# Eight blank products in place of thirty-one, and an order worked out anew with other lengths

## The chip, the cores and the metric

The kernel runs on one core of a Trainium2 chip. A core has a matrix engine (TensorE, PE in the profile), a vector engine (VectorE, DVE), a scalar engine (ScalarE, ACT), a general engine (GpSimd, POOL) and a queue engine that issues transfers (SyncE, SP). Each works through its own list of instructions strictly in that list's order; semaphores tie the lists together. The metric is the device time of one execution, in microseconds (us).

## The reference

Two stages follow each other. The first is attention in which each query may look only at some blocks of keys: q, k and v have 4 batches, 8 heads, 768 positions and 64 numbers each, in float32. Keys are grouped in 24 chunks of 32.

```python
k_min = np.min(k_chunks, axis=3); k_max = np.max(k_chunks, axis=3)
ub = np.sum(np.maximum(q * k_min, q * k_max), axis=-1)   # one bound per query and chunk
ub = np.where(causal, ub, -1e9)
top_chunks = np.argsort(ub, axis=-1)[..., -6:]           # six chunks per query
scores = np.where(selected & causal, (q @ k.T) / 8, -1e9)
attn = softmax(scores); out = attn @ v
```

The second takes the attention's result as x, 3072 rows of 512, and computes `g = elu(x @ w_in)` with 2048 columns and `g @ w_out`, which is the output.

## The kernel before, in words

The eight heads of a batch are four pairs, so there are 16 pairs, u0 to u15; two neighbouring pairs make a quad. Positions are split in two halves of 384, called hf 0 and hf 1. Work on one batch of the attention overlaps the products of the batch before it.

The pairs of batch 0 are prepared by `first_prep` (line 619). `load` (649) brings half a pair of keys or queries, 192 KB, in one transfer; eight products with the identity matrix turn it around in PSUM (`turn`, 668, the products of line 674); ScalarE copies it out (684, 702, 707), VectorE takes minimum and maximum of each chunk (690, 697), GpSimd casts the queries (724) and the values (715). Pairs of the later batches are prepared by `pair_prep` (562): four transfers of 96 KB each for keys and for queries (572), one of 384 KB for values (613), a transpose on VectorE (585, 603), minimum and maximum on VectorE (589), casts on GpSimd (724).

`quad_sel` (727) computes the bounds on TensorE (`ub`, 756), and VectorE finds each query's sixth largest bound and marks the chunks below it (773 to 796). GpSimd puts the marks below the queries (807), as further rows, so that the product of queries and keys (`sc`, 848) comes out already masked; each tile of keys carries 24 rows made from the constant `econ` for that (512). `pair_attend` (828) takes exponentials on ScalarE (875), masks the diagonal on GpSimd (894) or, early on, by a further product (854), multiplies by v (907), divides on VectorE (920, 923), transposes on TensorE (932) and copies the result to `xT` on ScalarE (935). `mlp` (939) multiplies by w_in, 16 blocks of 128 columns (`up`, 957), computes elu on ScalarE and VectorE (967 to 1001), and multiplies by w_out (`down`, 1020); ScalarE copies the result out and SP stores it (1028, 1032). The weights are brought by transfers that GpSimd issues (`weights`, 537, lines 541 and 545), each tied by `gates` to a step of the attention.

The order of all this isn't written by hand. Each step is handed to a `Plan` (128) with an engine, an assumed length, a priority, and what it reads and writes. `Plan.order` (191) first shifts the priorities by the list `RANKS` (first step, count, shift in fiftieths), and then lets a model of the engines and of the transfers take steps one by one: on each engine the step that can start first, and among those that can start at once the one of the lowest priority number. Buffers and PSUM banks are given out in the same pass. In the model, transfers stop in the stretches named in `STALLS` (140). The steps are then emitted in the order found, and that is the order of every engine's list. Where the assumed lengths differ from the chip's, the lists remain as they are, and an engine waits for whatever its next step lacks.

Ahead of all steps stand the blank products (lines 1081 to 1087): VectorE clears a tile, and TensorE multiplies it by itself into a PSUM bank that nobody reads.

The lines that the profile names are printed here.

Of the kernel before, what the change touches and what calls it, by code (L numbers as in the profile page):

```python
# [12 lines left out]
F32 = mybir.dt.float32  # L13
# [4 lines left out]
S = 768  # L18
# [23 lines left out]
def WHEN(q_in, left, out):  # L42
# [7 lines left out]
WARM = 31  # L50
# [5 lines left out]
RANKS = ((2, 1, 127), (6, 1, -127), (13, 1, -97), (17, 1, -112), (31, 1, -89), (35, 1, -71), (48, 1, -89),  # L56
# [62 lines left out]

DUMP = None  # L120


class Op:
    __slots__ = ("eng", "dur", "lat", "emit", "deps", "prio", "alloc", "free", "n", "users",
                 "left", "ready", "start", "end", "tag", "after", "followers", "port", "dma", "issues", "lane")


class Plan:
# [8 lines left out]
    COLD = 7.0  # L137
    RING = 2560
    LANES = 8
    STALLS = ((9.6, 11.7),)  # L140
    WAKE = 1.8

    def __init__(self, caps):
# [228 lines left out]
def kernel(  # L372
# [707 lines left out]
    with tc.manual_schedule():  # L1080
        if WARM:
# [4 lines left out]
            for _ in range(WARM):  # L1086
                nc.tensor.matmul(nothing, lhsT=blank, rhs=blank, start=True, stop=True)
# [34 lines left out]
```

## Time and profile before

| What | Value |
|---|---|
| Median of three runs | 276.94 us (276.51 to 277.29) |
| The profiled execution's own time | 276.84 us |
| Its span, first to last instruction | 275.1 us |
| TensorE busy | 264.6 us |
| VectorE busy | 202.0 us |
| ScalarE busy | 203.1 us |
| GpSimd busy | 127.4 us |
| Bytes moved by transfers | 29.82 MB |

1.7 us of the profiled execution lie outside the span. A row of the profile names a line of the kernel, an engine, an operation and its tiles; "idle before" is the time that the engine stood still just ahead of it, and the arrow names what ended that. Waits matter only on an engine that is the bound of its stretch. TensorE's records of neighbouring products overlap, because a product's end lies after the start of the next one.

### The profile page before, as it was taken

What the parts mean: (1) busy time and instruction counts of PE and PEld (TensorE: products, weight loads), DVE (VectorE), ACT (ScalarE), POOL (GpSimd) and SP (SyncE); (2) the same over time, 40 slices, a digit from 0 to 9 for tenths busy, and PEclk for the clock granted to TensorE, in tenths of its full rate; (3) what the DMA queues carried; (4) which work ended last, traced back from release to release, by engine and by line L of the source; (5) the groups of instructions that cost most, each with busy time, mean ns of one, the idle gap of its engine ahead of it and who ended that gap; (6) DMA issues with size and microseconds to landing.
All of it is one profiled execution on the core that took longest, in us unless ns stands there. A gap on an engine that the chain in (4) does not pass through costs nothing.

```text
span 275.1 us, 7274 instructions
## 1 busy us (share of the span) xinstructions
PE 264.6 (96%) x2751; PEld 164.7 (60%) x2751; DVE 202.0 (73%) x546; ACT 203.1 (74%) x382; POOL 127.4 (46%) x235
## 2 busy tenths in 40 slices
PE   8889899999999998999999999999999999999995
PEld 8778566565666564655566556665566755554544
DVE  5874979969999969999994775677965379374420
ACT  3879899948996898878999979964589844433311
POOL 5768565756997795968676164100162100000000
PEclk9999999999999999999999999999999999999999
DMA  7999999999999999999691010101020000210222
GB/s 184 240 222 230 174 165 179 158 160 156 191 156 151 173 149 179 196 158 174 94 212 42 2 38 2 38 0 41 1 80 0 28 13 2 77 38 2 76 76 76
DMA packets 111474, 29.82 MB, mean 108 GB/s; under 512 B 101072, under 2 KB 108496, under 8 KB 111440
## 3 DMA queue, kind: packets, MB, share of 16 engines
q1 hardware_dynamic: 106800, 24.78, 47.8%
q0 software_dynamic: 4224, 4.19, 9.6%
q8 instruction: 21, 0.34, 0.6%
q10 hardware_dynamic: 416, 0.39, 0.5%
q14 instruction: 13, 0.11, 0.1%
HBM read 27.26 MB, written 6.29 MB: 122 GB/s over the span
## 4 chain that ended last, share of the span: by engine, by line
PE 59%; DVE 21%; DMA 8%; ACT 5%; issue 3%; SPq 2%; POOL 1%; DVEq 0%; POOLq 0%
PE psM L1020 14%; PE psH L957 13%; PE psS L848 8%; PE psS L957 8%; PE psMT L1020 8%; DMA stage<-in_q_dram 5%; PE psO L907 4%; DVE thr L785 3%; DVE gT L975 2%; DVE qt L603 2%; SPq L572 2%; DVE selv L790 1%; ACT pt L875 1%; DVE gT L1001 1%; DVE ubt L773 1%
## 5 line engine op out<-in xcount | busy, mean ns | idle before, releaser
L875 ACT ACTIVATE pt<-psS 128x768 bf16<-128x768 f32 (+1 forms) x120 | 90.8, 789 | 5.8 <-PE psS L848 3.8
L957 PE MATMUL psH<-xT,w_in_sb 128*128 128x384 bf16 x384 | 74.0, 326 | 2.7 <-DVE gT L975 1.0
L1020 PE MATMUL psM<-w_out_sb,gT 128*128 128x512 bf16 x288 | 71.3, 379 | 0.0
L957 PEld LDWEIGHTS <-w_in_sb 128*128 128x128 bf16 x512 | 48.1, 97 | 38.1 <-issue 5.0
L967 ACT ACTIVATE e<-psH 128x384 f32<-128x384 f32 x96 | 48.1, 508 | 14.7 <-PE psH L957 14.1
L1020 PEld LDWEIGHTS <-gT 128*128 128x128 bf16 x400 | 37.4, 97 | 33.5
L894 POOL TENSOR_SCALAR_AFFINE_SELECT pt<-pt 128x256 bf16<-128x256 bf16 (+1 forms) x56 | 29.0, 522 | 57.3 <-ACT pt L875 56.2
L848 PE MATMUL psS<-rhs,lhs 88*128 88x384 bf16 (+4 forms) x304 | 52.5, 284 | 1.6 <-DVE ubt L773 0.6
L848 PEld LDWEIGHTS <-lhs 88*128 88x128 bf16 x304 | 27.4, 97 | 16.0 <-issue 2.1
L996 DVE SCALAR_TENSOR_TENSOR t<-e,psH 128x384 bf16<-128x384 f32 x48 | 25.7, 543 | 13.3 <-ACT e L967 13.2
L907 PEld LDWEIGHTS <-pt 128*128 128x128 bf16 x672 | 28.2, 98 | 6.7 <-issue 0.3
L724 POOL CAST rhs<-qt 64x768 bf16<-64x768 f32 (+1 forms) x40 | 27.7, 696 | 9.1 <-ACT qt L702 4.1
L807 POOL COPY rhs<-selt 24x192 bf16<-24x192 bf16 (+2 forms) x56 | 25.4, 455 | 13.6 <-DVE selt L796 9.5
L975 DVE SCALAR_TENSOR_TENSOR gT<-e,psH 128x384 bf16<-128x384 f32 x48 | 25.4, 535 | 8.0 <-ACT psH L972 7.3
L907 PE MATMUL psO<-vext,pt 128*128 128x65 bf16 x672 | 31.2, 194 | 0.0
L1001 DVE SCALAR_TENSOR_TENSOR gT<-psH,t 128x384 bf16<-128x384 f32 x48 | 25.9, 547 | 0.8
L967 ACT ACTIVATE e<-psS 128x768 f32<-128x768 f32 x16 | 13.0, 810 | 17.4 <-PE psS L957 17.4
L972 ACT ACTIVATE psH<-psH 128x384 f32<-128x384 f32 x48 | 24.7, 524 | 0.0
L957 PE MATMUL psS<-xT,w_in_sb 128*128 128x384 bf16 x128 | 23.1, 326 | 0.0
L1020 PE MATMUL psMT<-w_out_sb,gT 128*128 128x512 bf16 (+1 forms) x112 | 22.4, 349 | 0.0
L985 DVE TENSOR_SCALAR t<-e 128x768 bf16<-128x768 f32 x16 | 8.9, 559 | 16.8 <-ACT e L967 16.6
L724 POOL CAST lhs<-kt 64x768 bf16<-64x768 f32 x24 | 19.6, 818 | 2.0 <-PE psS L848 1.1
(66 smaller groups left out, 297.5 us busy)
## 6 DMA issues: line engine op xcount, KB each, us to landing
out_dram<-osb SPq DMA_DIRECT2D x23, 256.0 KB, 2.0
stage<-in_q_dram SPq DMA_DIRECT2D x48, 96.0 KB, 4.5
stage<-in_k_dram SPq DMA_DIRECT2D x48, 96.0 KB, 3.5
vd<-in_v_dram SPq DMA_DIRECT2D x12, 384.0 KB, 5.4
w_in_sb<-in_moe_w_in_dram POOLq DMA_DIRECT2D x4, 512.0 KB, 9.5
w_out_sb<-in_moe_w_out_dram POOLq DMA_DIRECT2D x4, 512.0 KB, 8.3
gT<-in_v_dram SPq DMA_DIRECT2D x16, 96.0 KB, 5.9
gT<-in_k_dram SPq DMA_DIRECT2D x6, 192.0 KB, 4.9
```

The source lines that it names most:

```text
L724: nc.gpsimd.tensor_copy(out=o, in_=i)
L807: eng.tensor_copy(out=dst.rearrange("c h (i two x) -> c h i two x", two=2, x=32)[:, :, :, odd, :], in_=tiles[st][r0:r0 + NCH, c0:c0 + n].r ...
L848: nc.tensor.matmul(p_s[:, hd, pc:pc + w], lhsT=tiles[pt_["kb"]][0:64 + NCH, hd, 128 * kb:128 * kb + 128], rhs=tiles[pt_["qb"]][0:64 + NCH, ...
L875: lambda bs=bs, pt=pt, wtot=wtot, lo=lo, at=at: nc.scalar.activation(out=tiles[pt][:, :, lo:lo + wtot], in_=tiles[bs[0]][:, :, at:at + wto ...
L894: nc.gpsimd.affine_select(out=a, in_=a, compare_op=AOT.is_ge, fill=0.0, base=0, pattern=pat, channel_multiplier=-1)
L907: nc.tensor.matmul(po[:, hd, qi, :], lhsT=tiles[pt][:, hd, off:off + 128], rhs=tiles[pt_["vx"]][:, 6 * hd + kb, :], start=(kb == 0), stop= ...
L957: nc.tensor.matmul(ph, lhsT=w_in_sb[:, kk, f0:f0 + 128], rhs=tiles[XT[4 * b + kk]][:, c0:c0 + HALF], start=(kk == 0), stop=(kk == NKK - 1))
L967: lambda e=e, view=view: nc.scalar.activation(out=tiles[e][:, 0:step], in_=view(), func=AF.Exp),
L975: lambda e=e, view=view, fc=fc, gt=gt: nc.vector.scalar_tensor_tensor(out=tiles[gt][:, fc:fc + step, :], in0=tiles[e][:, 0:step], scalar=1 ...
L996: lambda e=e, t=t, view=view: nc.vector.scalar_tensor_tensor(out=tiles[t][:, 0:step], in0=tiles[e][:, 0:step], scalar=1.0, in1=view(), op0 ...
L1001: lambda t=t, view=view, fc=fc, gt=gt: nc.vector.scalar_tensor_tensor(out=tiles[gt][:, fc:fc + step, :], in0=view(), scalar=0.0, in1=tiles ...
L1020: nc.tensor.matmul(pm, lhsT=tiles[gt][:, fc, 128 * tt:128 * tt + 128], rhs=w_out_sb[:, fc, cs], start=(fc == 0), stop=(fc == NFC - 1))
```

## The change

`WARM` is 8 in place of 31, and the blank products take 512 columns in place of 128, so the cleared tile grows from 128 to 512 columns and the bank's tile with it. The lengths that the plan assumes are altered for the early loads (issue 0.43 in place of 0.5, a half of keys or queries 0.069 in place of 0.062), for the values' casts, the bounds, and the products with w_in and w_out. The transfers' stops are put at five other times. `RANKS` is another list of shifts (386 entries before, 294 after, nearly all different). No step's own work is altered, and none is added or taken away beside the blank products.

```diff
-WARM = 31
+WARM = 8
-RANKS = ((2, 1, 127), (6, 1, -127), (13, 1, -97), (17, 1, -112), (31, 1, -89), (35, 1, -71), (48, 1, -89),
...
+RANKS = ((2, 1, -127), (4, 1, -23), (13, 1, -62), (15, 1, -90), (17, 1, -117), (19, 1, -127), (29, 1, -53),
...
-    STALLS = ((9.6, 11.7),)
+    STALLS = ((11.3, 13.0), (66.0, 67.0), (74.0, 75.0), (82.0, 82.6), (91.0, 91.6))
...
-        fetch(0.5, pl + 1.2, vload, [vd], (0.022, 1536, 1), alloc=[vd], reads=late)
-        add("POOL", 0.13 + 0.00084 * S, pr + 1.0,
+        fetch(0.43, pl + 1.2, vload, [vd], (0.022, 1536, 1), alloc=[vd], reads=late)
+        add("POOL", 0.14 + 0.00086 * S, pr + 1.0,
...
-        fetch(0.5, pl, load(at_k, kw, nc.sync), [(hk, i0)], (0.062, 192, 1), alloc=ak)
-        fetch(0.5, pl + 0.1, load(at_q, qw, nc.scalar if early else nc.sync), [(hq, i0 + 1)], (0.062, 192, 1),
+        fetch(0.43, pl, load(at_k, kw, nc.sync), [(hk, i0)], (0.069, 192, 1), alloc=ak)
+        fetch(0.43, pl + 0.1, load(at_q, qw, nc.scalar if early else nc.sync), [(hq, i0 + 1)], (0.069, 192, 1),
...
-        add("POOL", 0.13 + 0.00084 * HALF, pr + 1.0,
+        add("POOL", 0.14 + 0.00086 * HALF, pr + 1.0,
...
-        add("POOL", 0.13 + 0.00084 * w, pr, f, **kw)
+        add("POOL", 0.14 + 0.00086 * w, pr, f, **kw)
...
-            add("PE", 0.22 + 0.002 * n, pr, ub, reads=rd, writes=[bu[0]], alloc=bu, free=fr)
+            add("PE", 0.27 + 0.00166 * n, pr, ub, reads=rd, writes=[bu[0]], alloc=bu, free=fr)
...
-                add("PE", step * 4 * 0.1625, pr, up,
+                add("PE", step * 4 * 0.1618, pr, up,
...
-                        add("PE", 4 * (0.0033 + wide / 2400), pr, down,
+                        add("PE", 4 * (0.0024 + wide / 2400), pr, down,
...
-            blank = const.tile([P, P], BF16, name="blank")
-            nothing = psum.tile([P, P], F32, name="nothing", tag="bank3")
+            blank = const.tile([P, 512], BF16, name="blank")
+            nothing = psum.tile([P, 512], F32, name="nothing", tag="bank3")
             nc.vector.memset(blank, 0.0)
             for _ in range(WARM):
-                nc.tensor.matmul(nothing, lhsT=blank, rhs=blank, start=True, stop=True)
+                nc.tensor.matmul(nothing, lhsT=blank[:, 0:P], rhs=blank, start=True, stop=True)
```

What this does to each engine's list, as it comes out when both kernels are built:

- POOL, start: before, the identity (483) stands ahead of the two selections that make `econ` (500, 502); after, behind both of them. On VectorE the clearing of the query tiles (507) moves behind the three constants (474 to 476).
- SP, start: the third keys' load moves ahead of the first values and of the third queries. In the second half of batch 0 all keys and queries are loaded ahead of the last eight values' loads.
- POOL, batch 0: the cast of the third pair's values goes between the two casts of the fourth pair's queries.
- TensorE, batch 0: the turn of the queries of pair u2, second half, moves from the middle of the attention to just ahead of the first product with w_in.
- SP, batch 1: the four loads of u5's queries go ahead of the first 384 KB of values (613), not behind them.
- Batches 1 to 3: the order of keys' and queries' loads, of transposes and of products is different almost throughout. The bounds of u10 and u11 come 17.7 us of TensorE work later, those of u14 and u15 25.8 us of work earlier.

108 rows, old and new, of the table RANKS are left out of this document.

## The prediction

> **What bounds the kernel now.** I read the page first, then the busy time by stretches of 12 us, then the chain of waits, and last the order in time at the front and at three waits.
>
> ```profile
> span 275.1 us, 7274 instructions
> PE 264.6 (96%) x2751; PEld 164.7 (60%) x2751; DVE 202.0 (73%) x546; ACT 203.1 (74%) x382; POOL 127.4 (46%) x235
> DMA  7999999999999999999691010101020000210222
> PE 59%; DVE 21%; DMA 8%; ACT 5%; issue 3%; SPq 2%; POOL 1%; DVEq 0%; POOLq 0%
> ```
>
> TensorE is busy for 264.6 of 275.1 us, so 10.5 us of idle time is all that any order can win, and not all of that: the first product starts at 1.06 us and the last output's store follows the last product. The change leaves the work as it is. What it can do is move, shrink or enlarge these 10.5 us. The busy time by stretches (columns: stretch, length, busy and instructions of PE, its weight loads, DVE, ACT, POOL, clock, DMA share, GB/s) shows where they lie.
>
> ```profile
> 0.00:12.00 12.00, 10.10 (x155) 9.39 (x157) 8.80 (x27) 6.58 (x14) 7.62 (x26) 1.00 0.98 206
> 12.00:24.00 12.00, 10.88 (x247) 9.34 (x245) 7.96 (x37) 10.14 (x26) 9.06 (x19) 1.00 1.18 234
> 24.00:36.00 12.00, 11.07 (x155) 7.56 (x154) 8.91 (x34) 10.98 (x24) 8.14 (x17) 1.00 1.14 181
> 36.00:48.00 12.00, 11.13 (x145) 7.52 (x145) 11.17 (x35) 11.97 (x25) 6.95 (x14) 1.00 1.17 176
> 60.00:72.00 12.00, 11.68 (x126) 6.56 (x114) 11.26 (x42) 9.83 (x20) 9.05 (x17) 1.00 1.05 167
> 96.00:108.00 12.00, 11.12 (x166) 6.73 (x163) 8.92 (x38) 10.66 (x22) 8.78 (x13) 1.00 0.96 156
> 108.00:120.00 12.00, 11.65 (x163) 7.25 (x162) 11.88 (x32) 9.79 (x20) 10.09 (x17) 1.00 1.09 185
> 120.00:132.00 12.00, 11.35 (x77) 6.33 (x75) 11.94 (x33) 10.72 (x20) 8.96 (x19) 1.00 0.98 171
> ```
>
> ```profile
> 30.00:125.00 95.00, 91.32 (x1050) 55.69 (x1050) 86.03 (x256) 81.75 (x156) 70.19 (x121) 1.00 1.04 167
> ```
>
> TensorE stands still for 1.90, 1.12, 0.93 and 0.87 us in the first four stretches, 0.32 in 60 to 72, and 0.88, 0.35 and 0.65 in 96 to 132. From 132 us on there is no wait worth a line: TensorE then has more work waiting than it can do, and a better order wins nothing. Up to there the transfers are always busy, and VectorE nearly so; its one large gap (8.92 of 12) goes with the chain's wait for a load:
>
> ```profile
> 48.67 9.92 DMA stage<-in_q_dram
> ...
> 97.60 3.56 DMA stage<-in_k_dram
> ```
>
> **The change part by part.** The order is told by the two lists; "work ahead" is a count over a list, each instruction at its mean length in this profile.
>
> (1) The front: blanks, identity.
>
> ```profile
> 0.90 0.11 DVE L1085 MEMSET blank<- 128x64 uint32 x1 [0.90 <-PEq L1106]
> 1.06 3.49 PE L1087 MATMUL nothing<-blank 128*128 128x128 bf16 x31 [1.06 <-DVE blank L1085]
> 1.10 1.05 DVE L507 MEMSET rhs<- 32x192 uint32 x5
> ...
> 2.17 0.36 POOL L497 MEMSET vext<- 128x12 bf16 x5
> 2.46 0.29 POOL L483 TENSOR_SCALAR_AFFINE_SELECT ident_f<-ident_f 128x128 f32<-128x128 f32 x1
> 3.39 0.29 POOL L479 TENSOR_SCALAR_AFFINE_SELECT trineg<-trineg 128x128 bf16<-128x128 bf16 x1 [0.64 <-DVE trineg L476]
> 3.63 0.81 POOL L500 TENSOR_SCALAR_AFFINE_SELECT econ<-econ 32x768 bf16<-32x768 bf16 x1
> ...
> 4.48 1.55 PE L674 MATMUL psH<-ident_f,gT 96*64 96x96 f32 x16
> 4.52 0.81 POOL L502 TENSOR_SCALAR_AFFINE_SELECT econ<-econ 32x768 bf16<-32x768 bf16 x1
> 5.82 0.98 PE L674 MATMUL psMT<-ident_f,gT 96*64 96x96 f32 x16
> ```
>
> A memset of 64 elements takes 0.11 us, of 192 (1.05 by 5) 0.21; 256 make 0.26 by that line, so the blanks begin 0.15 later. 31 blanks of 128 columns fill 1.06 to 4.48, at most 0.11 each; eight of 512 at four times that make 3.5, which is as much. They end near 4.7. The identity now comes after two selections: the memsets ahead end at 2.5, the selections stand 0.89 apart, so 2.5 + 2 x 0.89 + 0.29 = 4.6. Both end near 4.7, and the first turn starts 0.3 later: **+0.3**. Ends: 0 (the first turn was held by its load) and +0.9 (the selections only start at 3.4, where the trineg selection of before still waited for VectorE).
>
> (2) The third keys' load comes three issues earlier on SP.
>
> ```profile
> 6.63 0.83 PE L674 MATMUL psH<-ident_f,gT 96*64 96x96 f32 x16
> ...
> 8.75 0.88 PE L674 MATMUL psH<-ident_f,gT 96*64 96x96 f32 x16 [0.63 <-ACT qt L702]
> 9.83 0.88 PE L674 MATMUL psMT<-ident_f,gT 96*64 96x96 f32 x16 [0.20 <-DVE kx L690]
> ```
>
> The named releaser of the 0.63 had long ended, so it was the load. This wait goes; behind it ScalarE, which copies each turn out, is the next to be late: its list has the same steps up to the first exponentials and starts later by (1). I take **-0.2**; ends 0 and -0.83 (both waits).
>
> One hole in the loads moves too. Of the early loads of 96 KB those issued at 6.9 to 8.5 land after 4.3 us, the one of 8.6 to 9.05 after 5.8 (transfers on those tiles by the stretch of their issue), and 8 to 14 us has one fetch of instructions in this queue (packets, MB, share):
>
> ```profile
> DMA to landing us min/median/max: 4.3/4.3/4.4
> ```
>
> ```profile
> DMA to landing us min/median/max: 5.7/5.8/5.9
> ```
>
> ```profile
> q8 instruction: 1, 0.02, 1.3%
> ```
>
> [...] Going by the row, 46 instructions fewer on TensorE (23 blanks with their weight loads), where a turn's 32 take 0.88 us, put the hole some 1.3 us later, behind the first keys of the second half instead of on values. Those are turned only after two scores: **0**; ends 0 and +0.8.
>
> (3) On POOL a cast of values (L715, 0.5 us) now stands between the two casts that the fourth pair's first scores need, and the bounds of that quad stand behind these scores on TensorE. In return the marks of the first pair are no longer split by such a cast. **0**; ends -0.5 and +0.5.
>
> (4) One turn (0.88) moves to just ahead of the first product with w_in.
>
> ```profile
> 28.65 0.88 PE L674 MATMUL psMT<-ident_f,kt 96*64 96x96 f32 x16 [0.31 <-ACT xT L935]
> 29.62 0.34 PE L932 MATMUL psT<-ident_b,on 128*128 128x128 bf16 x3
> 30.45 0.81 PE L957 MATMUL psH<-xT,w_in_sb 128*128 128x384 bf16 x4 [0.49 <-DVE kx L690]
> ```
>
> Between the transpose and the product, which wait on ScalarE's copy to xT, TensorE stands for 0.49; a turn of 0.88 fills that. **-0.5**; ends 0 and -0.8 (both waits).
>
> (5) u5's queries are issued ahead of 384 KB of values.
>
> ```profile
> 44.81 0.53 SPq L613 DMA_DIRECT2D vd<-in_v_dram  x1
> 45.44 12.82 SPq L572 DMA_DIRECT2D stage<-in_q_dram  x8
> ```
>
> ```profile
> 58.66 0.98 DVE L603 STREAM_TRANSPOSE qt<-stage 128x768 f32<-128x768 f32 x1 [1.53 <-DMA stage<-in_q_dram]
> ```
>
> This is the 9.92 of the chain. At 167 GB/s, 384 KB are 2.4 us. The transpose comes that much earlier, but TensorE is full in 48 to 60 and idle for only 0.32 in the next stretch. **-0.3**; ends 0 and -0.32. The values, behind the queries, are late next; nothing multiplies by them until that quad's scores.
>
> (6) Batches 1 and 2. The load waited for at 97.60 belongs to u10's keys. In the new lists it has 1.15 MB (7.1 us at 167 GB/s) more loads ahead, but 10.1 us more VectorE work ahead of its transpose: 3.0 us more cover, about what VectorE stood there (12 - 8.92 = 3.08). The bounds of u8 and u9's second half come 7.8 us, and u10 and u11's 17.7 us of TensorE work later. Against it: u8's keys lose 3.4 us of cover, u13's queries 7.1. The idle of 96 to 132 is 0.88 + 0.35 + 0.65 = 1.88. Most of these waits are products with w_in whose bank VectorE hasn't freed, and VectorE's total stays; so I take about half, **-1.0**; ends 0 and -1.88.
>
> (7) The rest. VectorE's preparation of u14 and u15 must be ready 25.8 us of TensorE work earlier; the count leaves 24 us of TensorE work over VectorE's there, where the tightest places have 10. In the end phase the products with w_in of the last half follow the last transpose after 0.86 us of other products, where (4) showed 30.45 - 29.62 = 0.83 needed. **+0.1**; ends 0 and +0.5. Shorter assumed lengths have no cost of their own.
>
> Sum: 0.3 - 0.2 + 0 + 0 - 0.5 - 0.3 - 1.0 + 0.1 = -1.6. On the profiled execution's own time, 276.84: **275.2 us**. That execution is 0.1 below the median of 276.94, so nothing is to be corrected. All low ends make -4.3, all high ends +3.0; both at once are unlikely.
>
> **The rivals.** *Nothing nets out, 276.8.* Up to 132 us VectorE is busy for 11.2 to 11.9 of 12 in most stretches; if it holds TensorE there by its sum of work, a wait that goes at one place comes back at the next one, and (4) to (6) are paid back. For it speaks that 86.03 of 95 are busy; against it, that TensorE's idle time is largest where VectorE too stands (96 to 108), so both wait for loads.
>
> *Slower, by the front, 277.8.* The identity comes after both selections; if they start at 3.4, the first turn starts at 5.4, +0.9. ScalarE is busy for 10.14 and 10.98 of 12 in the stretches after and passes the delay on up to the first product with w_in. With (4) and (2) used up by that, 276.84 + 0.9 = 277.8. It decides as soon as the identity comes after 5. Against it: VectorE's constants now come first, so the selections needn't wait for it.
>
> *Slower, by a load, 278.3.* Transposes of u8's keys or u13's queries reach the head of VectorE's list before their loads; behind them stand the steps that free the banks of the products with w_in. The like of it at 58.66 held VectorE for 1.53. In a stretch where TensorE has no other work that is 276.84 + 1.5. It decides where the 3.4 or 7.1 us of lost cover exceed what was there; by the count some 9 us remain.
>
> *The best case, 273.4:* (2), (4) and (6) at their low ends, 275.2 - 0.6 - 0.3 - 0.9 = 273.4.
>
> [...] The first turns of 16 products start at 4.48, 5.82 and 6.63, so 1.34 and 0.81 apart: the second ran faster. [...]
>
> **How the numbers follow.** Forecast, 274.4 to 276.0: 0.48. Best case: 0.08. Nothing nets out, 276.1 to 277.7: 0.20. The front: 0.14. A load: 0.10. A measurement of this kernel tells 0.3%, 0.83 us, from no change: faster means below 276.1. So faster 0.56, within 0.20, slower 0.24. The range takes in the best case and the load: 273.4 to 278.3.
>
> **What would show it.** (1) First turn near 4.8, identity at 4.6. (2) No wait of 0.6 at the fifth turn. (4) No wait of 0.49 ahead of the first product with w_in. (5) The last of u5's queries transposed by 56. (6) TensorE idle in 96 to 132 below 1.2, VectorE's gap in 96 to 108 smaller. The forecast is wrong if TensorE's idle time up to 132 us isn't below the 8 us or so of before, wherever it then lies.

## The result, and the profile after

The changed kernel takes 275.82 us (median of 22 runs, 274.56 to 280.48), the kernel before, run beside it, 277.79 (22 runs). The ratio is 0.9927, with a 95% interval of 0.9905 to 0.995: faster by 0.73%, some 2.0 us, where 1.6 were forecast. The profiled execution has 275.80 us with a span of 274.1, against 276.84 and 275.1, so the two traces compared here differ by 1.0 us only. Some executions of each kernel show a lower mean granted clock and last longer (the changed kernel's two longest, 280.48 and 280.46 us, have 0.988, where those under 276 have 0.998 to 1.000; one of the kernel before, beside a later run, 282.95 us at 0.962); the ratios leave most of them out.

First the page of the changed kernel: span, TensorE's busy time (matmuls and weight loads), and the summary of its chain of waits.

```profile
span 274.1 us, 7208 instructions
PE 263.4 (96%) x2705; PEld 163.0 (59%) x2728; DVE 200.4 (73%) x546; ACT 200.7 (73%) x382; POOL 127.7 (47%) x235
PE 80%; DMA 6%; ACT 3%; POOL 3%; DVE 3%; issue 2%; SPq 1%; ACTq 0%; POOLq 0%; DVEq 0%
```

VectorE's share of the chain fell from 21% to 3%. TensorE's busy time can't be compared directly: 2705 matmuls are on record beside 2728 weight loads, so the records of 23 matmuls are missing, and each may show as a small hole. The same stretches of 12 us as in the prediction:

```profile
24.00:36.00 12.00, 10.50 (x171) 7.14 (x175) 8.24 (x33) 10.48 (x23) 6.10 (x12) 1.00 1.09 180
48.00:60.00 12.00, 10.86 (x111) 6.83 (x110) 9.68 (x17) 10.29 (x20) 6.02 (x10) 1.00 1.11 175
96.00:108.00 12.00, 11.89 (x128) 7.14 (x127) 10.09 (x26) 11.17 (x22) 9.74 (x16) 1.00 1.04 177
108.00:120.00 12.00, 11.95 (x141) 7.76 (x140) 11.93 (x37) 10.18 (x22) 7.80 (x15) 1.00 1.19 170
120.00:132.00 12.00, 11.94 (x105) 7.24 (x104) 11.04 (x21) 12.00 (x24) 11.31 (x19) 1.00 1.14 163
```

In 96 to 132, where 1.88 us stood idle, 0.22 do. VectorE's gap in 96 to 108 is 1.91 where it was 3.08, and most of it, 1.79 at 103.01, is now a wait for TensorE and not for a load. But 48 to 60, which had none, has lost 1.14. The order in time shows where (TensorE, POOL, VectorE and a piece of the chain, sorted by start):

```profile
1.26 3.60 PE L1071 MATMUL nothing<-blank 128*128 128x512 bf16 x8 [1.26 <-DVE blank L1069]
4.17 0.28 POOL L467 TENSOR_SCALAR_AFFINE_SELECT ident_f<-ident_f 128x128 f32<-128x128 f32 x1
4.79 1.55 PE L658 MATMUL psH<-ident_f,gT 96*64 96x96 f32 x16
29.59 0.34 PE L916 MATMUL psT<-ident_b,on 128*128 128x128 bf16 x3 [0.83 <-DVE selv L774]
44.69 8.08 DMA stage<-in_k_dram
45.33 1.51 POOL L529 DMA_DIRECT2D w_out_sb<-in_moe_w_out_dram  x2
52.89 0.98 DVE L569 STREAM_TRANSPOSE kt<-stage 128x768 f32<-128x768 f32 x1 [1.24 <-DMA stage<-in_k_dram]
54.37 1.02 PE L1004 MATMUL psM<-w_out_sb,gT 128*128 128x512 bf16 x3 [0.96 <-DVE gT L985]
58.48 0.98 DVE L587 STREAM_TRANSPOSE qt<-stage 128x768 f32<-128x768 f32 x1 [0.40 <-DMA stage<-in_q_dram]
```

POOL issues the second pair of loads of w_out at 45.33, where the kernel before did so at 47.99. The last quarter of u5's keys, issued 0.64 us ahead of it at 44.69, lands only after 8.08 us. VectorE comes to the transpose of these keys, waits 1.24, and the step that makes gT stands behind it; TensorE waits 0.96 for that step.

To follow such losses through different orders I use one more number, the **shortfall**: the start of a weight load, less the length of all TensorE work that stands before it in the program. Lengths are those of packed runs in the traces: columns at 2.4 per ns and 2.5 ns more for each product, which gives the 0.65 of four with 384 columns (179.13 to 179.78 in the changed kernel) and the 0.86 of four with 512 (164.26 to 165.12), 0.032 us for a product with values, 0.83 for a turn (9.00 to 9.81), 0.39, 0.70 or 1.13 for a set of bounds. Where TensorE is full the shortfall stays level; what it grows is time lost. In us, by the time in the trace:

```
at (us)          25     50     60     92    124    132    268
before         4.57   8.15   8.31  10.85  14.40  14.55  15.37
changed        4.62   8.64  10.38  12.16  12.57  12.62  14.17
```

The change loses 2.07 by 60 us, wins 0.76 up to 92 and 3.24 from there to 132, and loses 0.73 after: 1.20 won in all. One trace stands for each kernel here, and two traces of one list can differ by microseconds, as k10_early below shows; so a shortfall is read for where it grows, and the ratios for what an edit is worth in all.

### The profile page after: what moved, and what is told of

Read it like the earlier page. It is cut to its first block, busy times and chain, and to the rows that moved or that the text cites. A ratio compares the mean times of both kernels' runs of the same rounds, so it can differ in the third digit from the quotient of the medians.

```text
span 274.1 us, 7208 instructions
## 1 busy us (share of the span) xinstructions
PE 263.4 (96%) x2705; PEld 163.0 (59%) x2728; DVE 200.4 (73%) x546; ACT 200.7 (73%) x382; POOL 127.7 (47%) x235
## 3 DMA queue, kind: packets, MB, share of 16 engines
q0 software_dynamic: 4224, 4.19, 9.5%
## 4 chain that ended last, share of the span: by engine, by line
PE 80%; DMA 6%; ACT 3%; POOL 3%; DVE 3%; issue 2%; SPq 1%; ACTq 0%; POOLq 0%; DVEq 0%
PE psM L1004 21%; PE psH L941 18%; PE psS L832 10%; PE psS L941 8%; PE psMT L1004 8%; PE psO L891 7%; PE psS L740 4%; DMA stage<-in_k_dram 3%; ACT pt L859 2%; DMA gT<-in_q_dram 2%; PE psT L916 2%; DMA gT<-in_k_dram 2%; PE psMT L658 1%; POOL lhs L708 1%; PE psH L658 1%
## 5 line engine op out<-in xcount | busy, mean ns | idle before, releaser
L1004 PE MATMUL psM<-w_out_sb,gT 128*128 128x512 bf16 x269 | 68.3, 379 | 2.0 <-DVE gT L985 1.0
L951 ACT ACTIVATE e<-psH 128x384 f32<-128x384 f32 x96 | 48.4, 524 | 10.6 <-PE psH L941 10.2
L791 POOL COPY rhs<-selt 24x192 bf16<-24x192 bf16 (+2 forms) x56 | 25.5, 456 | 16.4 <-DVE selt L780 13.8
L980 DVE SCALAR_TENSOR_TENSOR t<-e,psH 128x384 bf16<-128x384 f32 x48 | 25.8, 544 | 8.5 <-ACT e L951 8.5
L919 ACT ACTIVATE xT<-psT 128x384 bf16<-128x384 bf16 x32 | 16.4, 511 | 7.3 <-PE psT L916 7.3
```

The source lines that it names most:

```text
L791: eng.tensor_copy(out=dst.rearrange("c h (i two x) -> c h i two x", two=2, x=32)[:, :, :, odd, :], in_=tiles[st][r0:r0 + NCH, c0:c0 + n].r ...
L951: lambda e=e, view=view: nc.scalar.activation(out=tiles[e][:, 0:step], in_=view(), func=AF.Exp),
L980: lambda e=e, t=t, view=view: nc.vector.scalar_tensor_tensor(out=tiles[t][:, 0:step], in0=tiles[e][:, 0:step], scalar=1.0, in1=view(), op0 ...
L1004: nc.tensor.matmul(pm, lhsT=tiles[gt][:, fc, 128 * tt:128 * tt + 128], rhs=w_out_sb[:, fc, cs], start=(fc == 0), stop=(fc == NFC - 1))
```

## The experiments

Ratios are against the kernel before, run on the same chip, with 95% intervals. Where an order is rewritten, a list of operation numbers takes the place of the planner's walk; the rest of the kernel stays as it is. The new shifts and the new lengths can't be had apart: with old shifts and new lengths, or new shifts and old lengths, the planner comes to a point where no operation can start. So how much of the result belongs to either stays open.

**The two halves of the order exchanged at 58 us.**

```
- steps = plan.order()
+ steps = walk(plan, ORDER)   # front_before: before's list where start < 58, then the changed list
+                             # front_after: the changed list where start < 58, then before's
```

> The order of before up to 58 us of its plan, and what is left in the order of the changed kernel. Theory (the change wins some 3.3 us between 60 and 135 us and loses 2.2 between 40 and 58): ratio to before 0.985, about 273.6 us where the changed kernel has 275.8; TensorE waits in 48 to 60 as before, in 96 to 132 as the changed kernel. Rival (the gain comes from the front, the blanks aside): ratio 1.000, as before. Rival (only the whole order hangs together, loads out of step at the seam): slower than the changed kernel, ratio over 0.993.

> The reverse: the order of the changed kernel up to 58 us, and what is left in the order of before. Theory: the 2.2 us lost by 58 us stay lost and nothing is won later, ratio to before 1.008, and the waits of 96 to 132 are back (1.9 us). Rival (the gain comes from the front): ratio 0.993, as the changed kernel.

Measured: front_before 0.996 (0.9935 to 0.9985), front_after 1.0068 (1.0033 to 1.0102). The later part of the new order, seam included, is worth 0.4% behind the old front and 1.41% (1.0068 - 0.9927) behind its own; the new front by itself costs 0.68%. The 0.985 expected of front_before was a miss:

```
at (us)          25     50     60     92    124    132    268
front_before   4.58   8.26   9.50  12.47  13.06  13.11  14.72
front_after    4.62   8.47  11.55  13.94  15.59  16.00  16.77
```

From 92 to 132 us it loses 0.64, nearly as little as the changed kernel's 0.46, and front_after 2.06. That is less than the 3.70 of before, though each engine has the very list of before there. What differs is that the loads are in time: VectorE's waits of before for them (1.34 and 1.87; the first two lines) are gone, TensorE's of 0.29, 0.59 and 0.19 with them, and only the later ones are left (the third line is of front_after; before has the same 0.42 at 122.53).

```profile
97.02 0.98 DVE L603 STREAM_TRANSPOSE qt<-stage 128x768 f32<-128x768 f32 x1 [1.34 <-DMA stage<-in_q_dram]
101.24 0.98 DVE L585 STREAM_TRANSPOSE kt<-stage 128x768 f32<-128x768 f32 x1 [1.87 <-DMA stage<-in_k_dram]
124.04 1.46 PE L941 MATMUL psH<-xT,w_in_sb 128*128 128x384 bf16 x8 [0.42 <-DVE gT L985]
```

So 1.64 of the 3.24 won in this stretch can be had without the new list, from loads in time alone (here they are in time because all runs some 3 us later); the other 1.60 comes with the new list. But front_before was to keep the 8.31 of before at 60, and by 92 it is at 12.47. Its waits, on VectorE and TensorE:

```profile
58.63 0.98 DVE L587 STREAM_TRANSPOSE qt<-stage 128x768 f32<-128x768 f32 x1 [1.37 <-DMA stage<-in_q_dram]
60.35 0.34 PE L916 MATMUL psT<-ident_b,on 128*128 128x128 bf16 x3 [1.34 <-DVE on L907]
61.84 0.37 PE L740 MATMUL psS<-qa,km 64*32 64x96 f32 x8 [0.69 <-ACT qa L590]
```

The load of u5's queries is as late as in the kernel before (58.66, a wait of 1.53), where it cost TensorE nothing. At the seam a division that TensorE needs next stands behind it on VectorE, and TensorE waits 1.34: a front and a rest fit together only through their loads.

**The same exchange at 90 us.**

```
+ # changed_to_90: the changed list where start < 90, then before's; before_to_90 the reverse
```

> The order of the changed kernel up to 90 us of its plan, and what is left in the order of before. Theory (the win sits behind 90 us): TensorE stands 12.2 behind its work at 92 as in the changed kernel, and loses 4.5 more up to the end, as before did, where the changed kernel loses 2.0: ratio to before 1.001. Rival (the win sits between 58 and 90, or comes from the whole order): 0.993 to 0.996.

> The reverse: the order of before up to 90 us, what is left in the order of the changed kernel. Theory (the win sits behind 90 us and can be had without the loss at 55): TensorE 10.9 behind at 92 as before, and 2.0 more up to the end: ratio to before 0.988, 274.6. Rival (the later order needs the loads that its own first part has issued by then; the seam costs what is won): 0.994 or more, with new waits for loads between 90 and 110.

Measured: 1.0257 (1.0192 to 1.0321) and 1.0296 (1.0262 to 1.033). Both are far slower than either kernel, and the rival of before_to_90 stands. In changed_to_90 and then before_to_90 TensorE shows

```profile
104.85 1.44 PE L832 MATMUL psS<-rhs,lhs 88*128 88x384 bf16 x4 [5.42 <-POOL rhs L791]
```

```profile
100.27 0.34 PE L891 MATMUL psO<-vext,pt 128*128 128x65 bf16 x3 [4.34 <-POOL pt L878]
96.00:108.00 12.00, 7.27 (x49) 4.14 (x51) 7.12 (x13) 5.80 (x9) 6.36 (x12) 0.72 0.77 137
```

so nothing on the place of the win can be read from them; they show only what a seam costs where two lists differ in which pair comes next. Behind both long waits stand loads, as that rival has it: the chain of changed_to_90 goes back from POOL to a load of values, 5.66 us from 95.37, and in before_to_90 POOL waits 2.8 us for VectorE's transpose of queries, and that one 1.9 for its load.

**One transpose put back.** The place of the win needed a smaller cut. The changed kernel transposes u10's keys at 111.46 without a wait, 4 us after they land.

```
  VectorE's list: ..., ubt, gT,
+   kt of u10 (keys transposed),
    max, gT, selv, kt of u12, selt, gT, t, gT, gT, km of u12, t,
-   kt of u10,
    reciprocal, ...
```

> The changed kernel with one thing undone: VectorE's transpose of u10's keys moved ahead in its list past ten steps, to the place at 105.9, where their load (landing at 107.46) is not there yet, as in the kernel before; all loads as they are. Theory (the win between 92 and 132 us is VectorE no longer standing for loads ahead of steps that free the banks of products with w_in): VectorE waits 1.5 to 2 there, TensorE stands for gT about as long, is 1 to 2 us more behind at 124 us than 12.57, ratio to before 0.997 to 1.000. Rival (such a wait costs nothing by itself, VectorE's total or the order of its steps does): 0.993, TensorE at 124 us as the changed kernel.

Measured: 1.0089 (1.0052 to 1.0126). From 100 to 124 us its shortfall grows from 15.80 to 19.02, by 3.22, where the changed kernel's grows from 12.17 to 12.57. VectorE's wait and the one that follows on TensorE:

```profile
111.75 0.98 DVE L569 STREAM_TRANSPOSE kt<-stage 128x768 f32<-128x768 f32 x1 [1.93 <-DMA stage<-in_k_dram]
113.63 0.81 PE L941 MATMUL psH<-xT,w_in_sb 128*128 128x384 bf16 x4 [2.30 <-DVE gT L959]
```

One step of VectorE too early for its load, by 1.93, costs TensorE 2.30 at once, and 2.8 by 124 us (3.22 less the 0.40 of the changed kernel): the theory holds for the place, and the price is above the 1 to 2 expected. The ratio says more than the edit costs: this profile had lost 3.45 more than the changed kernel before 60 us, where the lists are the same (see the last section), so the ratio of 0.997 to 1.000 that was expected is missed, by a loss that this trace has ahead of the edit; why k10_early has it stays open. The reverse was tried on the kernel before:

```
  VectorE's list of before: ...,
-   kt of u10,
    ubt of u8 and u9,
-   km of u10,
    max of u8 and u9,
-   kx of u10,
    reciprocal, gT, on,
+   kt, km, kx of u10,
    gT, ...
```

On POOL the cast of these keys goes behind a cast of values with them, since it needs what VectorE makes.

> The kernel before with one move: VectorE's transpose of u10's keys and its two reductions behind seven other steps (bounds of u8 and u9, a division, products' steps) of its list, as the changed kernel has them later. Theory (the win of 92 to 132 us is VectorE no longer standing for loads): VectorE's wait of 1.87 at 101.2 shrinks below 0.5, TensorE's wait of 0.59 at 105.3 goes, ratio to before 0.995 to 0.997. Rival (VectorE's total, not the wait, holds TensorE there): ratio 1.000, the time comes back in waits for gT by 132.

Measured: 1.0102 (1.0045 to 1.0159), a miss. But most of what the trace lost was lost ahead of the move: at 50 us its shortfall is some 5.4 above that of before, in steps where the lists are the same, and TensorE's granted clock is down there (the figure ahead of the last two):

```profile
16.00:20.00 4.00, 4.00 (x76) 3.29 (x74) 2.26 (x13) 2.11 (x5) 2.18 (x6) 0.61 1.20 222
20.00:24.00 4.00, 4.00 (x42) 3.45 (x42) 1.64 (x6) 2.70 (x6) 1.44 (x4) 0.50 1.21 221
```

What the move itself does is read from 92 to 132 us, where the shortfall grows by 4.7 and that of before by 3.7: 1.0 lost, where a gain was expected.

```profile
109.60 0.97 DVE L585 STREAM_TRANSPOSE kt<-stage 128x768 f32<-128x768 f32 x1
112.93 0.81 PE L957 MATMUL psH<-xT,w_in_sb 128*128 128x384 bf16 x4 [1.99 <-DVE gT L975]
```

VectorE's wait of 1.87 for the load is gone, as expected. But the three steps (0.97, 0.95 and 0.94) now stand, by the place I chose, directly ahead of a step that makes gT, and TensorE waits 1.99 for that, where it waited 0.59. So it isn't enough that VectorE never waits for a load: at this place other work ahead of the step that frees the bank costs TensorE more than the wait did.

**The loss at 55: the loads of w_out.**

```
  POOL's list: ...,
-   second w_out pair,
    km of u4, mask, cast of u4's keys,
+   second w_out pair,
    casts of u4's queries, ...
```

> The changed kernel with the second pair of loads of w_out issued three of POOL's instructions later, at about 48.4 us where it is 45.3 (before: 48.0). Theory (this stream holds up the loads of u5's keys): the keys land 1 to 2 us earlier than 52.8, TensorE's wait of 0.96 at 54.4 goes, ratio to before 0.988. Rival (the keys' load is late by its own issue, or the products with the second half of w_out now wait): ratio 0.993 or more, and a wait of products with w_out for their load near 58.

Measured: 0.9908 (0.9876 to 0.994), and a span of 272.5. The pair is issued at 46.30, not at 48.4, but that is 2.2 us behind the last quarter of the keys (issued at 44.10) and is enough:

```profile
46.30 1.53 POOL L529 DMA_DIRECT2D w_out_sb<-in_moe_w_out_dram  x2
51.09 0.97 DVE L569 STREAM_TRANSPOSE kt<-stage 128x768 f32<-128x768 f32 x1
48.00:60.00 12.00, 11.87 (x152) 7.43 (x149) 9.86 (x19) 9.88 (x19) 6.67 (x10) 1.00 1.21 172
```

From issue to landing the last two quarters of u5's keys took, in the changed kernel (the first line) and here (the second),

```profile
DMA to landing us min/median/max: 3.7/5.9/8.1
```

```profile
DMA to landing us min/median/max: 4.0/4.0/4.1
```

and the shortfall at 60 us is 8.92 where the changed kernel has 10.38. No product with w_out waits for its load. In the profile it stays 1.5 ahead to the end (12.64 against 14.17); the timed runs don't tell 0.9908 from 0.9927. In w_out_turn below, with the same move, the last two quarters take 4.0 and 3.8 us.

**The step behind the late load.**

```
  VectorE's list: ..., t,
-   kt of u5, gT,
+   gT, kt of u5,
    reciprocal, ...
```

> The changed kernel with VectorE's transpose of u5's keys moved behind one step, the gT step that stood behind it in the list (loads as they are). Theory (the late load costs TensorE time only through this place in VectorE's list): the wait of 0.96 at 54.4 goes; TensorE at 60 us 0.5 to 1 us ahead of the changed kernel; ratio to before 0.990. Rival (up to 60 us the loads set the time, and the wait comes back at the next place): ratio 0.993, and the same 10.4 us behind its work at 60.

Measured: 0.9928 (0.9898 to 0.9958). The wait at 54.4 goes and comes back at the next place:

```profile
54.63 0.98 DVE L569 STREAM_TRANSPOSE kt<-stage 128x768 f32<-128x768 f32 x1 [1.83 <-DMA stage<-in_k_dram]
57.12 0.34 PE L916 MATMUL psT<-ident_b,on 128*128 128x128 bf16 x3 [1.10 <-DVE on L907]
```

The shortfall at 60 is 11.34, no better. The rival holds: the load is what has to be moved.

**The blanks alone.**

```
-WARM = 8
+WARM = 31
-                nc.tensor.matmul(nothing, lhsT=blank[:, 0:P], rhs=blank, ...)
+                nc.tensor.matmul(nothing[:, 0:P], lhsT=blank[:, 0:P], rhs=blank[:, 0:P], ...)
```

> The changed kernel with 31 blank products of 128 columns in place of eight of 512; everything else as it is. Theory (the same total of blanks, nothing else): ratio to before 0.993 and the first turn within 0.2 of 4.79. [...]

> The kernel with the later w_out loads, and 31 blank products of 128 in place of eight of 512. With 31 blanks the changed kernel stood 0.91 at 22.45, waiting for nothing the profile shows, and was 1.2 us later at 25 us, but lost that lead at 55 anyway. Theory (46 instructions more put an instruction fetch on TensorE's path there, and the load of u5's keys had hidden it): the same wait near 22, and now it reaches the end: ratio 0.995 where the eight blanks have 0.991. Rival (the blanks are worth nothing): 0.991.

Measured: 0.9937 (0.991 to 0.9964), and with the later w_out loads 0.9939 (0.9911 to 0.9967), where the eight blanks gave 0.9927 and 0.9908. The first turn is at 4.68. The end hardly moves, but the middle does: the shortfall of blanks_31 is 5.83 at 25 us, 9.78 at 50, and 10.46 at 60 beside the changed kernel's 4.62, 8.64 and 10.38. In blanks_31 TensorE has

```profile
22.45 0.32 PE L891 MATMUL psO<-vext,pt 128*128 128x65 bf16 x5 [0.91 <-issue]
```

a wait for nothing that the profile shows; w_out_blanks31 has it too (1.21 at 22.39), and the changed kernel has no such wait there. The traces don't tell what it is: from 18 to 23 us blanks_31 and the changed kernel have the same fetches of instructions, one packet on q8 and one on q14. The expectation that it would reach the end at 0.995 once the later w_out loads took its cover away is neither borne out nor excluded: the intervals overlap.

**The moved turn.**

```
  TensorE's list: turn of u3's queries,
+   turn of u2's queries,
    transpose (psT),
-   turn of u2's queries,
    first product with w_in, ...
```

> The changed kernel with the moved turn of u2's queries one place further ahead on TensorE, before the transpose that waits 0.83 at 29.6 for VectorE's division. Theory for the place: that wait is filled, the first product with w_in comes 0.7 earlier, at 30.0. Theory for the end (the loads of u5 hold the kernel at 55 us): ratio to before 0.993 all the same. Rival (gains before 55 us last): ratio 0.990.

> Two single moves on the changed kernel together: the second pair of w_out's loads three of POOL's instructions later, and the turn of u2's queries one place further ahead on TensorE. Theory: the late w_out keeps the keys' load ahead of the stream, so the 0.4 to 0.8 won at 30 us by the turn now last: ratio to before 0.989. Rival (what is won before 55 us is lost by 60 to the loads): 0.991, as with the later w_out alone.

Measured: 0.9941 (0.991 to 0.9972), and with the later w_out loads 0.9924 (0.9894 to 0.9954): no gain from either, and both theories for the place fell. In turn_ahead:

```profile
29.21 0.88 PE L658 MATMUL psMT<-ident_f,stage 96*64 96x96 f32 x16 [0.68 <-DVE selv L774]
30.95 2.11 PE L941 MATMUL psH<-xT,w_in_sb 128*128 128x384 bf16 x12 [0.58 <-ACT xT L919]
```

The turn waits for VectorE as well (until the step of line 774 ends at 29.03; its queries had landed by 20.8), so it is not work that was ready. And the product that it had covered now waits for ScalarE's copy again.

## Why the prediction was right, and where its terms were not

The total was right, -2.0 by the runs where -1.6 was forecast, but as a sum of terms that went wrong in both directions: a loss of 2.07 where -0.3 stood, and a gain of 3.24 where -1.0 stood. That they cancel so well is luck. Two of its sums don't come out of its own figures: the high ends add up to +2.7, not +3.0, and the idle time of before up to 132 us is 7.1, not "8 us or so". It set as its test that this idle time falls; it is 6.3 in the changed kernel.

(1) The front: right. Blanks to 4.86, the identity at 4.45 (4.17 + 0.28), the first turn at 4.79, 0.31 later. The rival of a slow front, which needed the identity behind 5, falls with that. (2) The wait ahead of the fifth turn is gone, though the seventh now waits 0.41 for its keys, at 10.81, and the shortfall at 20 us is 3.83 where before had 4.23: terms (1) and (2) together gave -0.4, not +0.1. The hole in the loads, costed at 0, cost nothing that the changed kernel's trace shows; no run shows that a fetch of instructions makes it, or that fewer instructions move it. The traces show q8's packet at 11.0 us before and at 13.8 in the changed kernel, 2.8 later where 1.3 was estimated, and the step up in the time to landing at the load of 96 KB issued at 8.63 before (from 4.3 to 5.7) and at one of 192 KB issued at 10.69 in the changed kernel (from 5.1 to 6.3). Part (2) put the hole into the loads alone, and blanks_31 has a wait of 0.91 on TensorE itself without a releaser. That this wait is a fetch of instructions is argued, from its coming with 46 more instructions; no row names it. (3) No wait that belongs to it was found.

(4) Failed. "A turn of 0.88 fills that": the wait of 0.49 ahead of the first product went, but 0.83 stands ahead of the transpose at 29.59, and that product starts at 30.68, not before the old 30.45. turn_ahead shows why: the turn isn't ready work, it waits for VectorE too.

(5) Failed, with the wrong sign. The last of u5's queries are transposed at 58.48, not by 56. The step counted what stands ahead on SP's queue only. The same new order issues the second w_out pair 2.7 us earlier, on POOL's queue, and beside that stream the keys' last quarter lands only after 8.1 us (4.0 to 4.1 in w_out_later), the queries after 7.1 to 8.2. POOL's queue was left out of that step. Instead of -0.3 the stretch to 60 us gave +2.07 by the shortfall. w_out_later, one trace, takes 1.46 of it back.

(6) Right in its mechanism, and far too small: -1.0 was taken, -3.24 came between 92 and 132 us. k10_early shows the mechanism by putting the wait back: VectorE's wait for a load becomes TensorE's wait for a bank, 1.93 to 2.30. front_after shows how much of the win it can be: without VectorE's waits for loads the list of before wins 1.64. The other 1.60 comes with the order of the new list, and which of its steps bring it wasn't followed. The cover came out at 4 us against a wait of 1.87 before, a gain of 5.9 where 3.0 was counted. The size failed for one more reason, in the measure: the term was half of the idle time in the 12-us rows, 1.88, and these rows hide part of each stop. Four products packed in a row take 0.65, the record of four ahead of a stop is 0.81 long, so each interrupted run counts 0.16 of standing still as busy. The shortfall of before grows by 3.70 from 92 to 132, twice what the rows call idle.

(7) +0.1 was taken, and 0.73 was lost after 132 us. A new wait of 0.32 for POOL's mask, at 152.09, is the largest piece; the rest is spread, and I didn't follow it.

```profile
152.09 0.75 PE L891 MATMUL psO<-vext,pt 128*128 128x65 bf16 x18 [0.32 <-POOL pt L878]
```

Of the rivals, "nothing nets out" had the right picture up to 60 us: k5_behind shows a wait that goes at one place and comes back at the next. It fails from 92 on, because there the limit is not VectorE's total (its 200.4 us busy are hardly fewer than the 202.0 of before) but the place of its waits and the order of its steps. The rival of a late load had the right mechanism and named the wrong loads: not u8's keys or u13's queries but u5's keys.

## What to carry to other kernels

Where an order is made anew, look at every queue at once: a bulk stream that another engine issues a microsecond or two earlier can cost as much as the waits that were planned away (1.46 of the 2.07 lost by 60 us here, by one trace). Moving that stream behind the small loads that are needed first took the wait away in two traces; in the timed runs the gain (0.9908 and 0.9924 against 0.9927) is within the noise. Size a win on a nearly full engine from its progress against its own work, not from idle time, which here hid 0.16 us of each stop and showed 1.88 where 3.70 was lost. And a wait of an in-order engine for a load can be paid by whoever waits for the steps behind it (VectorE's 1.93 became TensorE's 2.30 in k10_early); so put the steps that free another engine's buffers ahead of the step that may have to wait.

## What the runs showed of the hardware

In two traces a small load that met a bulk stream took about twice as long to land. The last quarter of u5's keys, 96 KB, takes 4.1 us when the w_out pair is issued 2.2 us later, 8.1 when it follows after 0.64, and in k10_early, where that quarter is issued at 46.26, behind the pair (45.41), the last two quarters take

```profile
DMA to landing us min/median/max: 8.5/8.6/8.6
```

The time of issue alone doesn't decide it: in turn_ahead that quarter is issued at 45.72, 0.11 behind the pair (45.61), and takes 4.1, and in blanks_31 at 45.85, 0.56 ahead of it, and takes 2.7. What else does is not shown. In the changed kernel the queue of the weights (q0, 4.19 MB in all, POOL's eight loads of 512 KB) and that of keys and queries (q1) have these packets (number, MB, share) from 48 to 50 us, where q1 has none, and from 51 to 53:

```profile
q0 software_dynamic: 346, 0.35, 106.4%
```

```profile
q0 software_dynamic: 378, 0.39, 113.5%
q1 hardware_dynamic: 380, 0.05, 29.9%
```

From 51 to 53 the two queues have about as many packets, and q1's carry an eighth of the bytes of q0's (0.05 MB beside 0.39). How the two share the transfer engines, and why q1 has no packet from 48 to 50, with the keys' last quarter on its way, is not shown.

Behind a long wait the granted clock can be lower. In the changed kernel TensorE waits 0.96 at 54.37, in front_after 2.18 at the same step, and the granted clock stays at 1.00 behind both. In k10_early, with the same order up to there, it waits 3.01, and the clock is 0.82 from 56 to 58 and 0.50 from 58 to 60:

```profile
56.48 1.13 PE L1004 MATMUL psM<-w_out_sb,gT 128*128 128x512 bf16 x4 [3.01 <-DVE gT L985]
56.00:58.00 2.00, 1.52 (x6) 0.69 (x6) 2.00 (x5) 0.00 (x0) 0.82 (x1) 0.82 1.21 189
58.00:60.00 2.00, 2.00 (x8) 0.86 (x7) 1.97 (x4) 0.81 (x1) 0.77 (x3) 0.50 0.56 88
```

The longer wait (3.01 - 0.96 = 2.05) and the clock (0.18 and 0.50 of 2 us each, 1.36) make up 3.41 of the 3.45 by which its shortfall at 60 us (13.83) exceeds the changed kernel's (10.38). But the length of one wait doesn't decide it. In before_to_90 the clock is at 0.50 from 43.4 to 46.8 us, behind a wait of 2.05 at 42.20, shorter than the 2.18 of front_after; in before_k10_later it is at 0.50 from 16.9 to 30.5, and no single wait between the first turn and that is above 0.82:

```profile
43.40:46.80 3.40, 3.40 (x12) 1.62 (x11) 3.36 (x17) 2.53 (x5) 0.06 (x1) 0.50 0.95 136
```

```profile
16.90:30.50 13.60, 13.60 (x171) 11.82 (x169) 5.15 (x21) 8.14 (x17) 7.70 (x17) 0.50 1.22 209
```

What lowers the clock is not shown. So the early w_out stream went with a loss of 0 (in blanks_31 the keys had landed in time) to over 3 us, if the lower clock behind the wait is counted to it, and lists that are the same up to there don't fix which.
